# Moving the one-hot products of a head pair to its last double step, with three PSUM banks in turn until the weight decode ends

## The chip, the core and the metric

The kernel runs on one core of one Trainium2 chip. The metric is the device time of one execution in microseconds; lower is better. Three runs of the kernel before gave 1151.7, 1154.13 and 1152.92 us, so the median is 1152.92 us.

## What is computed

The reference is a routed attention followed by a feed-forward block. Every query and key is assigned to the nearest of 16 centroids of its head, and attention is limited to pairs of the same cluster:

```python
q_assign = np.argmax(np.einsum('bhsd,hcd->bhsc', q_n, c_n), axis=-1)
k_assign = np.argmax(np.einsum('bhsd,hcd->bhsc', k_n, c_n), axis=-1)
mask = q_assign[:, :, :, None] == k_assign[:, :, None, :]
scores = np.where(mask, scale * np.matmul(q, k.transpose(0, 1, 3, 2)), -1000000000.0)
# softmax over the last axis, times v; heads side by side give x of 3072 x 512
h = x @ w_in
g = h * np.clip(h + 3.0, 0.0, 6.0) / 6.0
return (g @ w_out).astype(np.float32)
```

There are 4 batches, 8 heads, 768 positions of 64 elements; w_in is 512 x 2048 and w_out 2048 x 512. Both weights arrive in 8-byte floating point, and the kernel turns them into 4-byte numbers on the chip (the "decode").

## The kernel before

**Pairs and double steps.** Two heads are worked on together. There are 16 such pairs. One pair has 12 score steps: two halves of the queries (`hf`) times six chunks of 128 keys (`j`). The main loop goes through them two at a time: a *double step* is n = 0, 2, 4, ... up to 190, and r = n mod 12 is its place in its pair. In a double step TensorE makes the scores of steps n and n+1 into the PSUM tile `ps` (L354: first `ps<-xf`, the q-k product in 4-byte numbers, then `ps<-xm`, the mask product in bf16), ScalarE takes the exponential (`ex`, L366), POOL adds the exponentials into `acc` (L370, L373), and TensorE multiplies those of the double step before by v (`pv`, L383).

**Division.** At r=2 and r=8 the function `divide` sums `acc` over the keys on TensorE (`pd`, L404), and VectorE takes the reciprocal (`rcp`, L408) and multiplies (`xT`, L409). One double step later ScalarE makes two range sums from rcp (`same` L417, `lack` L419).

**Preparing the next pair.** While pair g runs, pair g+1 is prepared: at r=0 and 2 q and k are transposed (`turn`: `pqk` L278, copied to `xf` L280), at r=4 come the cluster scores (`pcs` L291, copied to `cs`), at r=6 `route` transposes them (`pr` L302) and VectorE finds the winners and writes `one_hot` (L306 to L322). Then `route_turn(g, part)` turns the one-hot rows with an identity into `po` (L334, four products into one PSUM bank) and copies them to a third of `xm` (L338). Part 0 holds query chunks 0 to 3, part 1 query chunks 4 and 5 and key chunks 0 and 1, part 2 key chunks 2 to 5. Parts 0 and 1 are made at r=8, part 2 at r=10; `xm` is read by the mask products of the next pair from its r=0 on.

**PSUM.** `ps` has four banks, `pv` one. The tile pool `psum_t` has one bank and `psum_m` two. Short-lived tiles (pc, pqk, pcs, pr, po, pd) come from `scratch`: while `st["early"]` holds, they go to `psum_m` and `psum_t` in turn, after that to `psum_t` alone. `early` ends at n = READY = 52. From n=54 on `psum_m` also holds the feed-forward tiles `ph` and `py`.

**Feed-forward items.** From n=54 on the list `fill` gives TensorE items of the feed-forward block: `up` items (eight ph products, L434; then `t` on ScalarE, L441, and `gT` on VectorE, L443) and `down` items (eight py products, L456; after the fourth part the copy `y`, L462, on VectorE). How many are taken in a double step is fixed by `items_by`. Up to n = DECODED = 96 that is none or one; in the steps from 96 to 103 the rest of the first half; later two or three. Within a double step items and preparation alternate, an item first.

**Decode.** 32 chunks of the weights are decoded. Each takes two sums on ScalarE (`wsize`, L208, L211) and five operations on VectorE (`wtop`, `wunit`, and `w_in_sb` or `w_out_sb`, L217 to L231). Up to n=48 one chunk is decoded in every five steps, from there one in every double step, at its end. The last is done at n=94.

**Order.** The whole order is written out by hand (`tc.manual_schedule()`): each engine works through its list in the order in which the program issues it.

Of the kernel before, what the change touches and what calls it, by code (L numbers as in the profile page):

```python
# [116 lines left out]
def fast_path(ctx, tc, ok, q, k, v, centroids, moe_w_in, moe_w_out, out):  # L117


    nc = tc.nc  # L120
# [44 lines left out]
    def scratch(shape, name):  # L165

        st["scratch"] += 1
        if st["early"] and st["scratch"] % 3:
            return psum_m.tile(shape, F32, name=name, tag="m")
        return psum_t.tile(shape, F32, name=name, tag="t")  # L170
# [3 lines left out]
    def load(g, *names):  # L174
        if g >= NPAIR:
            return
        b, h = divmod(2 * g, H)
        for name in names:
            if name == "v":
                dst = st["v", g] = vp.tile([P, NCH, 2, D], F32, name="vt")  # L180
            elif name == "q":
                st["qk", g] = qkp.tile([P, 2, NCH, 2, D], F32, name="qk")
            if name != "v":
                dst = st["qk", g][:, "qk".index(name)]
            src = {"q": q, "k": k, "v": v}[name]
            for t in range(2):
                nc.sync.dma_start(dst[:, :, t], src[b, h + t].rearrange("(p j) d -> p j d", p=P))
# [9 lines left out]
    def load_weights(i):  # L197
        if i < len(chunks):
            st["raw", i] = rawp.tile([P, WC, 2], U32, name="raw")
            nc.sync.dma_start(st["raw", i], chunks[i][1])  # L200
# [37 lines left out]
    def constants():  # L238
        make_identity(nc, ident)
        nc.vector.tensor_copy(out=ident_q, in_=ident)  # L240
        nc.vector.tensor_scalar_mul(out=ident_k, in0=ident, scalar1=-FAR)
        for t in range(2):
            nc.vector.tensor_reduce(
                out=parity[:, t : t + 1],
                in_=ident.rearrange("p (h t c) -> p t h c", t=2, c=C)[:, t], axis=AX.XY, op=ALU.max,
            )
        for c in range(C):
            nc.gpsimd.memset(rank[:, c : c + 1], float(C - c))
        nc.gpsimd.memset(half_c, 0.5)
        nc.gpsimd.memset(low_c, 1.0 / BOUND)  # L250
        nc.gpsimd.memset(ones, 1.0)
        nc.gpsimd.memset(w_low, W_LOW)
        nc.gpsimd.memset(one_hot, 0.0)
# [17 lines left out]
    def turn(g, part):  # L271
        if part == 0:
            st["xf", g] = xp.tile([P, NC2, P], F32, name="xf")
        qk, xf = st["qk", g], st["xf", g]
        pt = scratch([P, NHC, P], "pqk")
        for i in range(NHC):
            j = part * NHC + i
            nc.tensor.transpose(out=pt[:, i], in_=qk[:, j // NCH, j % NCH], identity=ident)  # L278
        dst = xf[:, part * NHC : (part + 1) * NHC]
        nc.scalar.copy(out=dst, in_=pt)  # L280
        if part == 3:
            st.pop(("qk", g))
# [4 lines left out]
    def cluster_scores(g):  # L287
        c0, xf = (2 * g) % H * C, st["xf", g]
        ps = scratch([P, 512], "pcs")[:, 0 : NC2 // 4 * P]
        for a in range(4):  # L290
            nc.tensor.matmul(  # L291
                ps[a * 2 * C : (a + 1) * 2 * C], lhsT=cnT[:, c0 : c0 + 2 * C], rhs=xf[:, a::4],
                start=True, stop=True,
            )
        cs = st["cs", g] = rtp.tile([P, NC2 // 4, P], F32, name="cs")
        nc.scalar.copy(out=cs, in_=ps)

    def route(g):
        cs = st.pop(("cs", g))
        pr = scratch([P, NC2, 2, C], "pr")  # L300
        for i in range(NC2 // 4):
            nc.tensor.transpose(out=pr[:, 4 * i : 4 * i + 4], in_=cs[:, i], identity=ident)  # L302
        shape = [P, 2 * NC2, C]
        pr = pr.rearrange("p j t c -> p (j t) c")
        mx = rtp.tile([P, 2 * NC2], F32, name="mx")
        nc.vector.reduce_max(out=mx, in_=pr, axis=AX.X)  # L306
        tie = rtp.tile(shape, F32, name="tie")
        nc.vector.tensor_tensor(
            out=tie, in0=pr, in1=mx.unsqueeze(2).to_broadcast(shape), op=ALU.is_ge
        )  # L310

        nc.vector.tensor_tensor(  # L312
            out=tie, in0=tie, in1=rank.unsqueeze(1).to_broadcast(shape), op=ALU.mult
        )
        first = rtp.tile([P, 2 * NC2], F32, name="first")
        nc.vector.reduce_max(out=first, in_=tie, axis=AX.X)
        oh = one_hot.rearrange("p j (t c) -> p j t c", t=2)
        tie = tie.rearrange("p (j t) c -> p j t c", t=2)
        first = first.rearrange("p (j t) -> p j t", t=2)
        for a, op in ((0, ALU.is_equal), (1, ALU.not_equal)):  # L320
            sl = slice(a * NCH, (a + 1) * NCH)
            nc.vector.tensor_tensor(  # L322
                out=oh[:, sl, :, 0:C], in0=tie[:, sl],
                in1=first[:, sl].unsqueeze(3).to_broadcast([P, NCH, 2, C]), op=op,
            )

    def route_turn(g, part):
        if part == 0:
            st["xm", g] = xp.tile([P, NC2, P], BF16, name="xm")
        xm = st["xm", g]  # L330
        po = scratch([P, 4, P], "po")
        for i in range(4):
            j = part * 4 + i
            nc.tensor.matmul(  # L334
                po[:, i], lhsT=one_hot[:, j], rhs=(ident_q if j < NCH else ident_k),
                start=True, stop=True,
            )
        nc.scalar.copy(out=xm[:, part * 4 : part * 4 + 4], in_=po)  # L338


    def where(n):
# [3 lines left out]
    def scores_qk(n):  # L345
        g, hf, j = where(n)
        st["ps", n] = psum_s.tile([P, 2, 512], F32, name="ps")
        scores_part(n, st["xf", g], True)
# [129 lines left out]
    def prep_items(g, r):  # L478

        if g >= NPAIR:  # L480
            return []
        if r in (0, 2):
            return [lambda: turn(g, r), lambda: turn(g, r + 1)]
        return {
            4: [lambda: cluster_scores(g)],
            6: [lambda: route(g)],
            8: [lambda: route_turn(g, 0), lambda: route_turn(g, 1)],
            10: [lambda: route_turn(g, 2)],
        }.get(r, [])

    per_pair = 2 * NCH
# [8 lines left out]
    READY = per_batch + lag_d  # L500
    DECODED = per_batch + 2 * (NW - per_batch // 5) + 2
# [19 lines left out]
    with tc.manual_schedule():  # L521
        nc.scalar.dma_start(cen, centroids.rearrange("h c d -> (h c) d"))
        load(0, "q", "k")
        constants()
        load(0, "v")
        load_weights(0)
        centroid_norm()
        for part in range(4):
            turn(0, part)
        load(1, "q", "k")  # L530
        scores_qk(0)
        scores_qk(1)
        cluster_scores(0)
        route(0)
        for part in range(3):
            route_turn(0, part)

        for n in range(0, total + lag_d + 2, 2):
            g, r = divmod(n, per_pair)
            for i in (n, n + 1):  # L540
                if i < total:
                    scores(i)
            for i in (n - lag_v, n - lag_v + 1):
                if 0 <= i < total:
                    attn_v(i)
            for check in later:
                check()
            later = []
            m = n - lag_d + 1
            if m >= 0 and m % NCH == NCH - 1:  # L550
                later.append(divide(m))
            prep = prep_items(g + 1, r)
            if r == 4 and prep:
                prep.pop()()
            if n == READY:
                st["early"] = False
            if m >= 0 and m % per_batch == per_batch - 1:
                fill += ffn_items(m // per_batch)
            if r == 6:
                load(g + 2, "q", "k")  # L560
                load(g + 1, "v")
            want = items_by(n + 2) - done if n < total else len(fill)
            want = min(want, len(fill))
            done += want
            for i in range(max(len(prep), want)):
                if i < want:
                    fill.pop(0)()
                if i < len(prep):
                    prep[i]()
            for i in range(chunks_by(n), chunks_by(n + 2)):  # L570
                load_weights(i + 1)
                decode_weights(i)
            if n >= total:
                for check in later:
                    check()
                later = []
# [5 lines left out]
    for got, sums, high in ((good, totals, BOUND), (fit, w_totals, W_HIGH)):  # L582
        for a, bound in enumerate((high, 0.0)):
            nc.vector.tensor_scalar(
                out=got[:, a], in0=sums[:, a], scalar1=bound, scalar2=None, op0=ALU.is_le
# [372 lines left out]
```

## Time and profile before

| | |
|---|---|
| median of three runs | 1152.92 us |
| the profiled execution | 1153.49 us |
| its span in the profile | 1151.4 us |
| mean granted TensorE clock | 0.976 |
| TensorE busy | 1084.7 us (94%) |
| VectorE busy | 390.3 us (34%) |
| ScalarE busy | 381.6 us (33%) |
| POOL busy | 300.5 us (26%) |
| HBM traffic over the span | 36 GB/s |

PE is TensorE's matmuls, PEld its weight loads, DVE is VectorE, ACT is ScalarE, POOL is GpSimd. In the page's second part the span is cut into 40 equal slices of 28.8 us, and a digit is the busy share of a slice in tenths; PEclk is the TensorE clock that was granted, in tenths of full speed. A row of waits names who waited on which line, for whom, then total us, times, and the longest. A row of a timeline has the start in us, the duration in us, the engine, the line, the operation, and in brackets the idle time before it with what ended it. A row of windows has the stretch, its length, then each engine's busy time.

### The profile page before, as it was taken

How to read it: one execution, taken by the hardware profiler on the slowest of the kernel's cores; microseconds unless marked ns; L12 is line 12 of the kernel's file. 1: busy time of each engine (PE TensorE's matmuls, PEld its weight loads, DVE VectorE, ACT ScalarE, POOL GpSimd, SP SyncE). 2: the span in 40 equal slices, each digit the busy share in tenths (PEclk: the TensorE clock that was granted, in tenths of full speed). 3: DMA queues.
4: the chain of work that ended last, by engine and by line, in shares of the span. 5: the costliest groups of instructions: out<-in, count | busy, mean ns of one | idle time of the engine just before them, and what ended most of it. 6: DMA issues, size and time to landing. Idle time of an engine off the chain costs nothing.

```text
span 1151.4 us, 11063 instructions
## 1 busy us (share of the span) xinstructions
PE 1084.7 (94%) x4402; PEld 520.9 (45%) x4402; DVE 390.3 (34%) x499; ACT 381.6 (33%) x740; POOL 300.5 (26%) x187
## 2 busy tenths in 40 slices
PE   6999969778799999999999999999999999999996
PEld 3444424333344554554445544454445544544542
DVE  3699995655901111222122211223112210210210
ACT  4667656444520310333214322243123320210210
POOL 2677734343311100332223223233113320000000
PEclk8999989898999999999999999999999999999999
DMA  4333244132300100020020202010000000000000
GB/s 113 84 96 93 71 115 115 56 96 73 78 10 19 41 1 19 10 42 1 10 59 1 42 10 51 10 42 1 10 24 9 1 1 27 1 9 19 1 9 22
DMA packets 83532, 42.77 MB, mean 37 GB/s; under 512 B 76304, under 2 KB 76304, under 8 KB 83472
## 3 DMA queue, kind: packets, MB, share of 16 engines
q1 hardware_dynamic: 83328, 41.95, 14.1%
q8 instruction: 36, 0.59, 0.2%
q14 instruction: 24, 0.20, 0.1%
q10 hardware_dynamic: 144, 0.03, 0.0%
HBM read 35.68 MB, written 6.29 MB: 36 GB/s over the span
## 4 chain that ended last, share of the span: by engine, by line
PE 86%; DVE 12%; ACT 1%; issue 0%; POOL 0%; DVEq 0%; POOLq 0%
PE py L456 29%; PE ph L434 29%; PE ps L354 13%; PE pv L383 10%; DVE rcp L408 2%; PE pqk L278 2%; DVE one_hot L322 2%; PE pd L404 1%; PE po L334 1%; DVE w_in_sb L231 1%; DVE wunit L228 1%; DVE wunit L224 1%; DVE wtop L221 1%; PE pcs L291 1%; DVE tie L312 1%; DVE wtop L217 1%
## 5 line engine op out<-in xcount | busy, mean ns | idle before, releaser
L373 POOL TENSOR_TENSOR acc<-acc,ex 128x768 f32<-128x768 f32 x128 | 237.5, 1856 | 452.8 <-ACT ex L366 447.7
L434 PE MATMUL ph<-xT,w_in_sb 128*128 128x384 f32 x1024 | 347.3, 491 | 0.7 <-DVE rcp L408 0.7
L456 PE MATMUL py<-w_out_sb,gT 128*128 128x512 f32 x768 | 338.7, 595 | 0.0
L434 PEld LDWEIGHTS ph<-xT,w_in_sb 128*128 128x128 f32 x1024 | 188.9, 190 | 146.0 <-issue 27.1
L456 PEld LDWEIGHTS py<-w_out_sb,gT 128*128 128x128 f32 x768 | 142.8, 190 | 176.4 <-issue 175.4
L366 ACT ACTIVATE ex<-ps 128x768 f32<-128x768 f32 x192 | 150.9, 806 | 180.3 <-PE ps L354 179.9
L441 ACT ACTIVATE t<-ph,half_c 128x384 f32<-128x384 f32 x128 | 74.4, 581 | 368.2 <-PE ph L434 368.2
L443 DVE SCALAR_TENSOR_TENSOR gT<-t,ph 128x384 f32<-128x384 f32 x128 | 70.9, 554 | 312.1 <-ACT t L441 312.1
L354 PE MATMUL ps<-xf 64*128 64x384 f32 x768 | 175.8, 537 | 0.6 <-ACT ex L366 0.6
L383 PE MATMUL pv<-ex,vt 128*64 128x384 f32 x768 | 147.9, 507 | 0.0
L462 DVE COPY y<-py 128x512 f32<-128x512 f32 x24 | 16.6, 691 | 289.6 <-PE py L456 289.6
L370 POOL TENSOR_TENSOR acc<-ex 128x768 f32<-128x768 f32 x32 | 60.3, 1884 | 182.0 <-ACT ex L366 182.0
L408 DVE RECIPROCAL rcp<-pd 128x384 f32<-128x384 f32 x32 | 81.7, 2555 | 75.4 <-PE pd L404 75.3
L354 PEld LDWEIGHTS ps<-xf 64*128 64x128 f32 x768 | 67.0, 196 | 59.0 <-issue 42.3
L383 PEld LDWEIGHTS pv<-ex,vt 128*64 128x64 f32 x768 | 47.5, 139 | 85.2 <-issue 82.8
L354 PE MATMUL ps<-xm 64*128 64x384 bf16 x384 | 66.0, 338 | 0.7 <-ACT xm L338 0.7
L280 ACT COPY xf<-pqk 128x384 f32<-128x384 f32 x64 | 29.6, 479 | 77.1 <-PE pqk L278 77.1
L338 ACT CAST xm<-po 128x512 bf16<-128x512 f32 x48 | 27.4, 582 | 59.0 <-PE po L334 59.0
L334 PE MATMUL po<-ident_q,one_hot 128*128 128x128 bf16 x96 | 11.3, 244 | 37.6 <-DVE rcp L408 24.3
L334 PEld LDWEIGHTS <-one_hot 128*128 128x128 bf16 x192 | 14.6, 105 | 57.5 <-issue 37.4
L278 PE MATMUL pqk<-ident,qk 128*128 128x128 f32 x192 | 32.5, 293 | 6.6 <-ACT xf L280 3.9
L278 PEld LDWEIGHTS pqk<-ident,qk 128*128 128x128 f32 x192 | 24.1, 149 | 29.4 <-issue 14.2
(70 smaller groups left out, 460.2 us busy)
## 6 DMA issues: line engine op xcount, KB each, us to landing
raw<-in_moe_w_in_dram SPq DMA_DIRECT2D x16, 512.0 KB, 3.7
raw<-in_moe_w_out_dram SPq DMA_DIRECT2D x16, 512.0 KB, 3.5
qk<-in_q_dram SPq DMA_DIRECT2D x32, 192.0 KB, 3.4
qk<-in_k_dram SPq DMA_DIRECT2D x32, 192.0 KB, 4.1
vt<-in_v_dram SPq DMA_DIRECT2D x32, 192.0 KB, 4.1
out_dram<-y SPq DMA_DIRECT2D x24, 256.0 KB, 2.0
cen<-in_centroids_dram ACTq DMA_DIRECT2D x1, 32.0 KB, 1.8
```

Of the source, the lines that this page charges most:

```text
L278: nc.tensor.transpose(out=pt[:, i], in_=qk[:, j // NCH, j % NCH], identity=ident)
L334: nc.tensor.matmul(po[:, i], lhsT=one_hot[:, j], rhs=(ident_q if j < NCH else ident_k), start=True, stop=True,)
L354: nc.tensor.matmul(st["ps", n][:, t, 0:HALF], lhsT=x[r, NCH + j], rhs=x[r, hf * NHC : (hf + 1) * NHC], start=first, stop=not first,)
L366: nc.scalar.activation(out=ex, in_=sc, func=ACT.Exp, scale=SM_SCALE)
L370: nc.gpsimd.tensor_tensor(out=acc, in0=st["ex", n - 1], in1=ex, op=ALU.add)
L373: nc.gpsimd.tensor_tensor(out=acc, in0=acc, in1=ex, op=ALU.add)
L383: nc.tensor.matmul(pv[t * D : (t + 1) * D], lhsT=vt[:, j, t], rhs=ex[:, t], start=(j == 0), stop=(j == NCH - 1),)
L408: nc.vector.reciprocal(out=rcp, in_=pd)
L434: nc.tensor.matmul(hh, lhsT=w_in_sb[:, kt, f * P : (f + 1) * P], rhs=xT[:, kt, hf * HALF : (hf + 1) * HALF], start=(kt == 0), stop=(kt == ...
L441: nc.scalar.activation(out=t, in_=hh, func=ACT.Relu, bias=half_c, scale=1.0 / 6.0)
L443: nc.vector.scalar_tensor_tensor(out=gT, in0=t, scalar=1.0, in1=hh, op0=ALU.min, op1=ALU.mult)
L456: nc.tensor.matmul(py, lhsT=st["g", f][:, i * P : (i + 1) * P], rhs=w_out_sb[:, f], start=(f == 0), stop=(f == NFT - 1),)
```

## The change

Three things are edited. `route_turn` is called for all three parts at r=10, and for none at r=8. The copy of part 1 goes to VectorE; those of parts 0 and 2 stay on ScalarE. And `early` ends at n = DECODED (96) instead of READY (52), so that scratch tiles go round three banks for that much longer, in which the feed-forward tiles use two of them too. The call of all three parts for the first pair, ahead of the loop, gets VectorE's copy as well.

```diff
                 po[:, i], lhsT=one_hot[:, j], rhs=(ident_q if j < NCH else ident_k),
                 start=True, stop=True,
             )
-        nc.scalar.copy(out=xm[:, part * 4 : part * 4 + 4], in_=po)
+        dst = xm[:, part * 4 : part * 4 + 4]
+        if part == 1:
+            nc.vector.tensor_copy(out=dst, in_=po)
+        else:
+            nc.scalar.copy(out=dst, in_=po)
...
             6: [lambda: route(g)],
-            8: [lambda: route_turn(g, 0), lambda: route_turn(g, 1)],
-            10: [lambda: route_turn(g, 2)],
+            10: [lambda: route_turn(g, 0), lambda: route_turn(g, 1), lambda: route_turn(g, 2)],
         }.get(r, [])
...
-            if n == READY:
+            if n == DECODED:
                 st["early"] = False
```

## The prediction

> **What bounds the kernel now.** I read the busy table and the 40 slices first, then TensorE's waits, then the windows by stage, then the timeline at the pair boundaries, where the change acts.
>
> ```profile
> PE 1084.7 (94%) x4402; PEld 520.9 (45%) x4402; DVE 390.3 (34%) x499; ACT 381.6 (33%) x740; POOL 300.5 (26%) x187
> PE   6999969778799999999999999999999999999996
> DVE  3699995655901111222122211223112210210210
> PEclk8999989898999999999999999999999999999999
> ```
> TensorE is full from slice 11 on. Before that it has holes, VectorE is the busy neighbour, and the granted clock dips after each hole.
>
> ```profile
> PE po L334 <- DVE rcp L408: 24.3, 4, 8.1
> PE po L334 <- DVE one_hot L322: 12.0, 6, 3.0
> PE pqk L278 <- ACT xf L280: 3.9, 6, 0.7
> PE po L334 <- ACT xm L338: 2.7, 4, 0.7
> PE pqk L278 <- DVE rcp L408: 2.7, 1, 2.7
> ```
> All waits of size concern the scratch tiles. These windows put them in stages (span, PE busy, DVE busy, ACT, POOL, PEclk):
>
> ```profile
> 36.00:129.30 93.30, 84.26 (x539) 37.65 (x539) 85.68 (x74) 63.35 (x131) 63.49 (x33) 0.96 0.31 78
> 172.90:322.70 149.80, 122.46 (x605) 57.79 (x602) 97.35 (x134) 80.30 (x176) 55.74 (x31) 0.91 0.30 80
> 322.70:1140.00 817.30, 817.30 (x2938) 396.74 (x2935) 151.34 (x216) 195.01 (x350) 144.99 (x80) 1.00 0.07 17
> ```
> So before 323 us a removed hole is time won. After 323 us TensorE has no hole at all, and any new one is time lost.
>
> I name double steps by n (0, 2, ...); counting the ps groups puts n=12 at 45.7 us, 24 at 74.5, 36 at 101.6, 48 at 128.6, 60 at 172.1, 72 at 220.1, 84 at 273.5, 96 at 321.9. A boundary is the scores of n=12, 24, ...: their xm product needs parts 0 and 1, while part 2 is wanted one step later. So today part 2 alone is made in the last step, and nothing waits for it.
>
> **The change, stage by stage.** It adds no arithmetic: 16 of 48 copies go from ScalarE (582 ns) to VectorE. The nearest row is `y<-py`, a VectorE copy of 128x512 out of PSUM, 691 ns. I take 0.69 us (0.58 would change the sum by 1 us). No DMA is moved, and SP and POOL get the same lists. Behind the moved copy VectorE has that step's decode and the next rcp, behind ScalarE's copies come the decode's sums and the next exp; where part 1's products are late, these wait too, which no row shows: 0 while TensorE is the late one anyway, at most one copy (0.7 us) at a boundary.
>
> *Boundaries 108 to 180, after the decode (7 pairs).* One bank is left for scratch tiles here, and each of these last steps has two FFN items. Built, the order is item, part 0, item, part 1, part 2: nothing stands between part 1's copy and part 2's products in the same bank. Scores and the rest of TensorE's list queue behind that wait.
>
> ```profile
> 478.26 0.39 PE L334 MATMUL po<-ident_k,one_hot 128*128 128x128 bf16 x4
> 478.46 0.58 ACT L441 ACTIVATE t<-ph,half_c 128x384 f32<-128x384 f32 x1 [2.25 <-PE ph L434]
> 479.07 0.55 DVE L443 SCALAR_TENSOR_TENSOR gT<-t,ph 128x384 f32<-128x384 f32 x1 [5.70 <-ACT t L441]
> ```
> In 4 of the 7 pairs the second item is an `up`. VectorE takes its gT first: products start at 0, gT ends at 1.36, the copy ends at 2.08, TensorE resumes at 2.14 instead of 0.32: 1.8 us. In 3 pairs it is a `down` part without a copy: 0.39 + 0.03 + 0.69 + 0.05 - 0.32 = 0.85. Sum 4 x 1.8 + 3 x 0.85 = 9.8 us, all on the path; at r=8 nothing was lost before, so nothing comes back.
>
> The clock adds to it. These two slices say where it drops:
>
> ```profile
> 38.00:41.40 3.40, 1.78 (x18) 1.06 (x18) 3.40 (x3) 1.44 (x3) 1.88 (x2) 1.00 0.00 0
> 41.40:44.80 3.40, 3.40 (x14) 1.20 (x12) 3.26 (x4) 3.37 (x9) 1.33 (x1) 0.50 0.00 0
> ```
> A 3.4 us slice in which TensorE was busy 1.78 us is followed by one at half clock; the slice 96.0 to 99.4, busy 1.96, is not. An `up` wait of 1.75 us idle, if it falls nearly whole into one such slice (about 57 in 100), leaves 1.66 busy, and the next slice costs half of 3.4 us: 4 x 0.57 x 1.7 = 3.9 us (0 to 6.8). Stage sum +13.7.
>
> The Trainium skill, "TensorE: Matmul & The Clock Gate", section "Why this matters for your kernels", says otherwise: only idle gaps above about 3 us should cost the clock. By it this term is 0 and the whole sum 3.9 us lower. The slice above had 1.62 us of idle, split in two, so I follow the row.
>
> *Boundaries 12, 24, 36 (before the FFN).* The one_hot waits at r=8 (12.0 less 3.0 at the start) vanish: po comes a step later. But xm now waits for the last step's copies, and both engines reach them late. ScalarE has same and lack (L417, L419) ahead, which need rcp: part 0 is copied 1.8 us after rcp ends (74.50 to 76.22 in the trace). VectorE has rcp, xT and, at 12, one decode ahead.
>
> ```profile
> 40.09 2.54 DVE L408 RECIPROCAL rcp<-pd 128x384 f32<-128x384 f32 x1
> 43.67 2.19 DVE L221 SCALAR_TENSOR_TENSOR wtop<-raw,wtop 128x512 uint32<-128x512 uint32 x1
> 45.89 1.91 DVE L224 TENSOR_SCALAR wunit<-wtop 128x512 uint32<-128x512 uint32 x1
> ```
> The two decode ops above stretch from 0.69 and 0.43 because POOL's additions run beside them (43.47 to 47.52). A decode takes 2.9 us alone, and about 1.5 more for each op so blocked.
> - 12: rcp ends 42.63, xT waits for POOL until 44.4, decode to 47.3, copy to 48.05, against 46.42 today: +1.6 (0.6 with no block). The idle brings one half-clock slice: +1.5.
> - 24: the decode before rcp ran unblocked (68.98 to 72.03) because the one_hot wait had starved POOL. Without that wait the additions fall on it: rcp ends 74.5 to 77.5, xm follows 1.8 later, 76.3 to 79.3 against 75.26: +1.0 to +4.1. I take 3.0, nearer the blocked rows as POOL will be running, and 1.4 for the clock.
> - 36: rcp ends 100.12, xm 101.9 to 102.25, against 102.33: 0.
> Sum +7.5 (1.6 to 8.6). The start wins 0.2: two copies run side by side.
>
> *Boundaries 48 and 60.* At 48 rcp ends 127.1; xT, a decode and the copy put xm at 131.5 to 132.2, against 129.32. At 60 VectorE is one unbroken chain. Today xm follows the end of rcp by 8.5 us; then by xT 0.56 + gT 0.55 + decode 2.9 + copy 0.7 + gaps = 4.85, so -3.65 if rcp stays. It does not: TensorE comes 5 us late out of 48 (wait and half clock), and POOL blocks decodes that now run beside it, about +4.7. I take +1 (-3.6 to +4).
>
> *Boundaries 72, 84, 96: the gain.* The po <- rcp waits vanish at r=8.
>
> ```profile
> 204.98 0.41 DVE L217 TENSOR_SCALAR wtop<-raw 128x512 uint32<-128x512 uint32 x1
> 207.96 2.55 DVE L408 RECIPROCAL rcp<-pd 128x384 f32<-128x384 f32 x1
> 210.56 0.58 PE L334 MATMUL po<-ident_q,one_hot 128*128 128x128 bf16 x4 [5.24 <-DVE rcp L408]
> 220.86 0.33 PE L354 MATMUL ps<-xm 64*128 64x384 bf16 x2
> ```
> From the end of rcp to xm today: 10.35, 11.4, 10.8 us. After: xT, gT, decode, gT, copy = 5.4, 4.85, 5.4. That is -17.0 if rcp stays. But exp and POOL's additions now run while VectorE decodes ahead of rcp; by the blocked rows this moves rcp by 1.8, 3.2, 1.7: +6.7. New idle before each boundary (on gT or rcp, whose bank a scratch tile or an `up` now shares) brings half clock again: 0.5 + 2.0 + 1.8 = +4.3. The three banks also free the turns: pqk waits of 0.7, 0.6, 3.3 and 1.2 go, with one half-clock slice (1.2): -7.0. Sum -13.0 (-24 with no block, -8 with three more blocked ops).
>
> **Sum.** 13.7 + 7.5 - 0.2 + 1.0 - 13.0 = +9.0 us. The profiled execution took 1153.49 us, of which the span is 1151.4; the shown median is 1152.92, so I predict 1162 us. Ends: 9.8 + 1.6 - 0.2 - 3.6 - 24 = -16.4, and 16.6 + 8.6 - 0.2 + 4 - 8 = +21.
>
> **Rivals.**
> - *VectorE keeps up (faster).* One mechanism: whether POOL's additions block the decode ops at 48 to 96. If they don't, the gain is 24 + 3.6 and 24 costs only 1.0: -24 - 3.6 + 13.7 + 1.6 + 2.9 - 0.2 = -9.6, 1143 us. I count ten such blocks (1 at 12, 2 at 24, 3 at 60, 1, 2 and 1 later); between 9.0 and -9.6 the sign turns where about half of them stay away. For it: VectorE is idle 35% of 172.9 to 322.7. Against: the stretched rows recur wherever POOL is busy. Chance 0.18.
> - *Wash.* Stage gain 22 against the same losses: within 0.2%, 2.3 us, which is about what a measurement of this kernel can tell from no change. Chance 0.08.
> - *Heavier.* `up` tiles share two banks with scratch tiles, so ph waits for a gT that sits behind a decode; each of five boundaries loses another 2 to 3 us with its clock slice: +20, 1173 us. For it: the built order puts three ph in a row into one bank at n=60 to 64. Against: gT there had idle time before it (5 to 7 us). Chance 0.19.
> - *The change doesn't do what it says*: excluded by the built order; the tiles stand in three banks up to n=94, and part 1's copy stands on VectorE 16 times.
> My forecast (1153 to 1168): 0.55. The range for 8 in 10 reaches from 1146, which leaves out most of the first rival's own spread, to 1174. Faster by over 0.2%: 0.17; within: 0.09; slower: 0.74.
>
> **What would show it.** In the waits, po <- rcp falls from 24.3 to under 8 us, po <- one_hot to about 3 (the start), and new rows stand: ps or po <- VectorE's xm copy, near 10 us after 323 us (po, 7 times, four near 1.8) and more before. The span from the scores of n=60 to those of 96 shrinks from 150 to about 137 us, that from 12 to 48 grows by about 5. PEclk shows single dips after slice 11. I am wrong if the late po waits are near 0.2 us, if the clock doesn't dip beside them, or if decode ops keep their 0.4 and 0.7 us while POOL is busy.

## The result and the profile after

The changed kernel takes 1160.92 us (median of 4 runs, 1159.53 to 1162.33) against 1152.31 us for the kernel before beside it (4 runs, 1150.65 to 1154.13): 1.0074 times as long, 95% interval 1.0054 to 1.0095. Its profiled execution took 1162.33 us, with a span of 1160.4 us and a mean granted clock of 0.971.

First the busy table and the 40 slices of the page after; a slice is 29.0 us here.

```profile
PE 1088.9 (94%) x4402; PEld 522.7 (45%) x4402; DVE 398.4 (34%) x515; ACT 375.0 (32%) x724; POOL 300.7 (26%) x187
PE   6879897997999999999999999999999999999996
DVE  4497777877901120222122301323112210210210
PEclk9889998998999999999999999999999999999999
```

VectorE has 16 instructions more, ScalarE 16 fewer: the moved copies. The holes of TensorE are still in the first eleven slices. After them the granted clock is full until the last 6 us, though the waits below say that new holes stand there. Those of TensorE's waits that concern the moved products (who waited on which line, for whom, total us, times, longest):

```profile
PE po L334 <- DVE rcp L412: 21.2, 6, 6.8
PE ps L358 <- DVE xm L340: 10.5, 5, 4.0
PE po L334 <- DVE xm L340: 8.9, 7, 1.6
PE po L334 <- DVE gT L447: 5.0, 2, 3.5
PE po L334 <- DVE one_hot L322: 4.4, 3, 3.0
```

The one_hot row shrank to little more than the start (from 12.0). The rcp row hardly did (from 24.3). Two rows on VectorE's copy of `xm` are new: one for the scores (ps), with 3.99 us at 12, 3.86 at 48 and three short ones, and one for part 2's products (po) after 323 us, seven times.

How much each boundary moved is read from the first exp of double step n in both timelines (us, after minus before):

| n | 12 | 24 | 36 | 48 | 60 | 72 | 84 | 96 | 108 | 132 | 156 | 180 |
|---|---|---|---|---|---|---|---|---|---|---|---|---|
| difference | +0.6 | +7.3 | +11.0 | +15.4 | +11.3 | +7.3 | +1.8 | -1.0 | +0.7 | +3.2 | +5.8 | +8.3 |

So the change loses 15.4 us up to the scores of n=48, wins 16.4 from there to 96, and loses 9.3 again from 96 to 180. The last 0.7 us of the 9.0 by which the span grew come after the last exp. Single boundaries are known less well than to the tenth: e1 below runs the program of before up to n=52 and is 2.2 us earlier at 48, and e3 below runs that of after up to 96 and is 3.8 us earlier there. Differences of that size are not the edit's.

The timeline at one of the four late boundaries with an `up` item:

```profile
479.77 0.58 ACT L445 ACTIVATE t<-ph,half_c 128x384 f32<-128x384 f32 x1 [1.80 <-PE ph L438]
480.38 0.56 DVE L447 SCALAR_TENSOR_TENSOR gT<-t,ph 128x384 f32<-128x384 f32 x1 [2.30 <-ACT t L445]
480.85 0.68 DVE L340 CAST xm<-po 128x512 bf16<-128x512 f32 x1
481.59 0.38 PE L334 MATMUL po<-ident_k,one_hot 128*128 128x128 bf16 x4 [1.64 <-DVE xm L340]
```

VectorE's list has gT ahead of the copy, gT waits for ScalarE's `t`, and part 2's products wait 1.64 us for the one bank. And two early boundaries, 24 (above the dots) and 12 (below):

```profile
78.27 2.55 DVE L412 RECIPROCAL rcp<-pd 128x384 f32<-128x384 f32 x1
80.85 0.52 ACT L421 ACTIVATE same<-rcp 128x384 bf16<-128x384 f32 x1 [8.93 <-DVE rcp L412]
80.87 0.59 PE L334 MATMUL po<-ident_k,one_hot 128*128 128x128 bf16 x4 [6.76 <-DVE rcp L412]
81.97 1.05 ACT L342 CAST xm<-po 128x512 bf16<-128x512 f32 x2
...
46.09 0.68 DVE L340 CAST xm<-po 128x512 bf16<-128x512 f32 x1
46.83 0.50 PE L358 MATMUL ps<-xm 64*128 64x384 bf16 x2 [3.99 <-DVE xm L340]
```

At 24 two things stand behind the same rcp at once: TensorE's products of part 2, whose bank the denominators `pd` hold until rcp has read it, and ScalarE's `same` and `lack`, with the copies of parts 0 and 2 in line after them. At 12 the scores wait 3.99 us for the VectorE copy, which stands behind a whole decode.

### The profile page after: what moved, and what is told of

It reads as the page before. It is cut to its first block, busy times and chain, and to the rows that moved or that the text cites. A ratio compares the mean times of both kernels' runs of the same rounds, so it can differ in the third digit from the quotient of the medians.

```text
span 1160.4 us, 11063 instructions
## 1 busy us (share of the span) xinstructions
PE 1088.9 (94%) x4402; PEld 522.7 (45%) x4402; DVE 398.4 (34%) x515; ACT 375.0 (32%) x724; POOL 300.7 (26%) x187
## 3 DMA queue, kind: packets, MB, share of 16 engines
q1 hardware_dynamic: 83328, 41.95, 14.1%
## 4 chain that ended last, share of the span: by engine, by line
PE 82%; DVE 16%; ACT 1%; issue 0%; POOL 0%; DVEq 0%; POOLq 0%
PE py L460 29%; PE ph L438 28%; PE ps L358 11%; PE pv L387 9%; DVE rcp L412 3%; DVE one_hot L322 2%; PE pqk L278 2%; DVE wunit L228 2%; PE pd L408 1%; DVE wtop L221 1%; DVE wunit L224 1%; DVE w_in_sb L231 1%; DVE wtop L217 1%; DVE xT L413 1%; DVE tie L312 1%; PE pcs L291 1%
## 5 line engine op out<-in xcount | busy, mean ns | idle before, releaser
L387 PE MATMUL pv<-ex,vt 128*64 128x384 f32 x768 | 151.7, 518 | 0.0
L358 PEld LDWEIGHTS <-xm 64*128 64x128 bf16 x384 | 20.0, 97 | 40.6 <-DVE xm L340 14.8
L334 PE MATMUL po<-ident_k,one_hot 128*128 128x128 bf16 x96 | 11.5, 238 | 25.6 <-DVE rcp L412 11.0
```

Of the source, the lines that this page charges most:

```text
L358: nc.tensor.matmul(st["ps", n][:, t, 0:HALF], lhsT=x[r, NCH + j], rhs=x[r, hf * NHC : (hf + 1) * NHC], start=first, stop=not first,)
L387: nc.tensor.matmul(pv[t * D : (t + 1) * D], lhsT=vt[:, j, t], rhs=ex[:, t], start=(j == 0), stop=(j == NCH - 1),)
```

## The experiments

**Which part of the change does what (e1, e2).** The three edits come apart: three banks without the move and the VectorE copy, and the other way round.

```diff
e1, from the kernel before:
-            if n == READY:
+            if n == DECODED:
e2, from the kernel after:
-            if n == DECODED:
+            if n == READY:
```

> The kernel before with one edit alone: scratch tiles go round three banks until n=96; the one-hot products stay at r=8, 8 and 10, and all copies on ScalarE. As built, part 0 has another bank than pd at n=68 and 80 and the same one at n=56 and 92. Theory (the po waits on rcp before 323 us are a matter of the bank that pd holds): two of the four waits (5.2 and 8.1 us at 68 and 80) shrink to a wait on one_hot of 0 to 2.6 us, the other two stay, the pqk waits shrink: about 1142 us (1135 to 1147). Rival (VectorE's chain sets the pace whatever the banks are, and the wait comes back on ps, ph or xm): within 4 us of 1152. After 323 us no new wait in either.

> The changed kernel without the banks: all three parts at r=10 and part 1's copy on VectorE, but scratch tiles have one bank from n=52 on. Theory: the losses at boundaries 12 to 36 (11.0 us in the changed kernel) and after 323 us (9.3 us) stay as they are; from 48 to 96 the three parts go through one bank one after the other, part 2 behind a VectorE copy that stands behind a decode, so the gain of 12.3 us shrinks to 3 to 9: about 1166 us (1160 to 1171). Rival (the gain comes from the move to r=10 and not from the banks): the gain stays, 1158 to 1162 us.

Measured: e1 1131.35 us, 0.982 times the kernel before (0.9804 to 0.9836); e2 1175.12 us, 1.0199 times (1.0184 to 1.0215). Before is 1152.77 in this group. The signs were right and both sizes far too small: the banks alone win 21 us where 11 were expected, the move with its copy loses 22 where 13 were. The banks carry nearly all of the gain, and the move takes it back: with the banks given, it costs 1160.92 - 1131.35 = 29.6 us. Between 60 and 96, where the move was to pay, e2 wins 0.9 us. In e1's waits:

```profile
PE po L334 <- DVE one_hot L322: 14.2, 8, 3.0
PE po L334 <- DVE rcp L408: 12.9, 2, 7.6
PE pqk L278 <- DVE rcp L408: 0.9, 1, 0.9
PE pqk L278 <- ACT xf L280: 0.7, 1, 0.7
```

Two of the four rcp waits are gone without any move, since the other turns of the three banks do not meet `pd`.

**Where by stage (e3, e4).** The change stands only for the pairs for which COND holds; all others have the old order of the products and ScalarE's copies. g is the pair prepared, and the code is shortened.

```diff
+            8: [] if COND else [part 0, part 1],
+            10: [all three parts] if COND else [part 2],
...
+        if part == 1 and COND:
             nc.vector.tensor_copy(out=dst, in_=po)
e3: COND is g < 9       e4: COND is 5 <= g < 9
```

> The changed kernel, with the schedule of before (parts 0 and 1 at r=8, part 2 at r=10, ScalarE's copies) for the seven pairs prepared after n=96. Theory: the 9.3 us that the changed kernel loses from step 96 to step 180 are the seven waits of part 2's products on part 1's VectorE copy and nothing else; they go: 1151.6 us (1150 to 1153), and from the scores of step 96 to those of step 180 it takes what before took, 558.6 us. Rival (part of the loss is a later state of the pipeline, carried in from the first stages): 1153 to 1157 us.

> The new schedule and VectorE's copy only for the four pairs prepared from n=48 to 94 (boundaries 60, 72, 84, 96), the schedule of before for all others, three banks until n=96. Theory (stages add up): the 11.0 us at 12 to 36 and the 4.4 us at 48 are not lost, the 9.3 us after 323 us are not lost, and the gain of 12.3 us at 72 to 96 stays; boundary 60, which won 4.1 us after a late 48, gives 0 to 4: about 1138 us (1135 to 1143). Rival (the gain at 72 to 96 is in part the early losses given back, since VectorE had drained its decodes by then): 1144 to 1152 us.

Measured: e3 1151.01 us (0.9984, 0.9972 to 0.9996), e4 1137.69 us (0.9876, 0.9858 to 0.9894). The median falls by 9.9 us, where 9.3 were told, and e3's timeline shows nothing lost from 96 to 180 (-4.77 against before at both), so the late boundaries cost what the timeline said, 9.3. e4 is a hit too, but e1 without any move is 6.3 us faster still: where the move was thought to pay, the banks were paying.

**What in the move costs (e5, e6, e7).** Three steps, each on top of the one before: part 1's copy back on ScalarE; part 2 kept out of pd's bank at the boundaries 12 to 48 (`own` names the pool); `same` and `lack` issued after the products and copies.

```diff
e5:
-        if part == 1:
-            nc.vector.tensor_copy(out=dst, in_=po)
-        else:
-            nc.scalar.copy(out=dst, in_=po)
+        nc.scalar.copy(out=dst, in_=po)
e6, too:
+        own = {1: "t", 2: "t", 3: "m", 4: "t"}.get(g) if part == 2 else None
+        po = scratch([P, 4, P], "po", own)
e7, too:
-            for check in later:
-                check()
-            later = []
+            due, later = later, []
...
             for i in range(max(len(prep), want)):
...
+            for check in due:
+                check()
```

> The change with part 1's copy put back on ScalarE; banks and the move to r=10 stay. Theory VectorE-copy: the copy stands behind the rows that VectorE has queued (decode at boundaries 12 and 48, gT at the late up boundaries), so the scores' wait of 3.99 us at 12 falls to about 1.4 and the one of 3.86 us at 48 likewise (some 2.6 us each and up to 1.4 of half clock each), late up waits fall from 1.7 to about 1.15 and down waits from 0.85 to 0.75 (4 x 0.55 + 3 x 0.1 = 2.5 us): 1160.9 - 8.5 = 1152.5 (1150 to 1156). Rival, the move alone: all three parts stand after rcp and behind ScalarE's same and lack, whatever engine copies part 1: 1159.5 to 1161.5. Both expect boundary 24 to keep its 6.8 us wait.

> As e5, and part 2's products of pairs 12 to 48 are kept out of the bank that the denominators pd use. Theory bank: what holds boundaries 24 and 36 is that bank (waits for rcp of 6.76 and 2.18 us), so they lose 8 to 9 us less than with e5: 1144 (1142 to 1147). Rival, ScalarE's queue: the copies stand behind same and lack, which wait for the same rcp, so the wait only turns from po to ps (ps for xm): within 1.5 us of e5, 1151 to 1154. I lean to the rival: in the trace of the change the xm copies at boundary 24 come at 81.97, behind same at 80.85 and lack at 81.37.

> As e6, and same and lack are issued after the step's products and copies, so nothing between the products and the scores waits for rcp at the early boundaries. Both theories of e6 are cured: boundaries 12 to 48 go at least as early as in the kernel before (differences of 0 to -2 us), 1160.9 - 8.5 (e5) - 9 = about 1141 (1137 to 1145), with the late boundaries still +6.9 us over before. If the move itself costs by something else (one_hot blocked by POOL, VectorE being late), it stays above 1148.

Measured, with before at 1152.5: e5 1144.85 us (0.9941, 0.9926 to 0.9956); e6 1150.1 (0.9987, 0.9977 to 0.9996); e7 1133.82 (0.9835, 0.9815 to 0.9856; its five runs lie from 1130.78 to 1137.38). By boundary, against before (the profiled executions):

| n | 12 | 24 | 36 | 48 | 60 | 72 | 84 | 96 | 180 |
|---|---|---|---|---|---|---|---|---|---|
| after | +0.6 | +7.3 | +11.0 | +15.4 | +11.3 | +7.3 | +1.8 | -1.0 | +8.3 |
| e5 | -2.3 | +2.2 | +5.6 | +8.1 | +2.9 | -2.5 | -9.7 | -15.1 | -9.0 |
| e6 | -3.2 | +3.3 | +7.0 | +11.3 | +4.3 | -0.9 | -8.2 | -13.6 | -7.5 |
| e7 | -2.8 | -0.5 | -0.1 | -1.5 | -6.0 | -11.6 | -18.5 | -22.0 | -15.9 |
| e1 | -2.0 | -2.3 | -2.2 | -2.2 | -4.1 | -8.8 | -21.9 | -23.0 | -23.0 |

e5: the VectorE copy costs 16.1 us in all, twice what was expected, and the move with ScalarE's copies the other 13.5 (1144.85 - 1131.35). In the profiled runs e5 is 14.1 us ahead of the change by n=96, most boundaries adding 1 to 3 us, and gains 3.2 more late. At a late `up` boundary ScalarE's copy has only `t` ahead of it, and the wait is 0.92 instead of 1.64 us:

```profile
465.65 0.58 ACT L442 ACTIVATE t<-ph,half_c 128x384 f32<-128x384 f32 x1 [1.80 <-PE ph L435]
466.13 0.58 ACT L339 CAST xm<-po 128x512 bf16<-128x512 f32 x1
466.76 0.38 PE L334 MATMUL po<-ident_k,one_hot 128*128 128x128 bf16 x4 [0.92 <-ACT xm L339]
```

e6 settles between the two causes at 24 and 36. The bank theory (1144) falls: out of pd's bank the wait stays and changes its name, as the copies themselves stand behind `same` and `lack`. The same two waits in e5 (the first two rows) and in e6 (the last two); the 9.0 us are those at 24:

```profile
PE po L334 <- DVE rcp L409: 21.9, 6, 6.8
PE po L334 <- ACT xm L339: 7.1, 9, 0.9
PE po L335 <- ACT xm L340: 26.3, 13, 9.0
PE po L335 <- DVE rcp L410: 8.4, 2, 4.9
```

Its median is 5.2 us above e5's, more than the 1.5 allowed, while its profiled execution (1146.42 us) is only 1.5 above; that difference is left open. e7 then takes the sums out of the way, and the loss of +7.0 at 36 goes to -0.1. It came out 7 us better than expected; e5, on which the sum was built, had already come out 8 us better. Of the 12.8 us by which e7 is ahead of e6 at 48, 8.4 are left at 96. So at the early boundaries ScalarE's list, with the sums ahead of the copies, is enough by itself to hold the loss; whether pd's bank alone would hold it too was not tried. e7's late boundaries still lose 6.1 us, which is what sets it behind e1 in the table.

**Whether e1's two remaining rcp waits can go (e8, e12).** e8 keeps the products of the pairs at 60 and 96 in the bank that pd doesn't use; e12 holds the decode issued at r=6 back until after the denominators of r=8.

```diff
e8, from e1:
+        po = scratch([P, 4, P], "po", g in (5, 8))    # True: psum_t
e12, from e1:
+            if held and r != 6:
+                decode_weights(held.pop())
             for i in range(chunks_by(n), chunks_by(n + 2)):
                 load_weights(i + 1)
-                decode_weights(i)
+                if r == 6:
+                    held.append(i)
+                else:
+                    decode_weights(i)
```

> e1 (the kernel before with three banks until DECODED, no move, no VectorE copy) with the products of pairs 60 and 96 kept in the bank that pd does not use: there e1 still waits for rcp 7.58 and 5.36 us. Theory bank: both waits go, and only the copy between parts of one bank (0.7 us each) stays: 1131.3 less 6 to 11 us = 1123 (1120 to 1126). Rival, VectorE is what is late in that stage: the wait comes back at the next gT, pqk or pd, 1129 to 1132.

> e1 with the decode that is issued at r = 6, between one_hot and rcp on VectorE, held back until after the denominators of r = 8. Theory rcp behind the decode: the two waits po for rcp of e1 (7.6 and 5.3 us) shrink by the 2.9 us of a decode each, and the half-clock slices behind them by some: 1131.4 - 5.8 - 0 to 3 = 1124 (1121 to 1127). Rival, VectorE is full there whatever the order: the wait comes back at gT, pd or pqk, 1129 to 1133.

Measured: e8 1131.63 us (0.9822, 0.9805 to 0.9838), no different from e1. The two waits of po for rcp are gone, and this stands in their place:

```profile
PE pqk L278 <- DVE rcp L408: 8.6, 2, 4.6
```

The rival fits: the wait for VectorE comes back under another name, and nothing is won. e12 took 1139.07 us (0.9887, 0.9872 to 0.9902), worse than e1 and outside of both expectations. Its po for rcp did fall, from 12.9 to 3.0 us, but its decode became slower: the five operations of a chunk sum to 5.10 us in the mean between 36 and 322 us, against 4.58 in e1. Of the 155 decode operations there 45 take 1.5 us or more, against 34 in e1. That two chunks in a row now run beside POOL's additions, and that this costs the 8 us, was argued, not tried.

**Whether POOL's additions stretch the decode (e10, e11).** The kernels before and after without the additions for j over 1, so that the softmax denominators lack four of the six key chunks; only their times count here.

```diff
-        elif j > 1:
-            acc = st["acc", g, hf]
-            nc.gpsimd.tensor_tensor(out=acc, in0=acc, in1=ex, op=ALU.add)
```

> The kernel before without GpSimd's additions of the exponentials for j over 1 (the softmax denominator is then the sum of the first two key tiles only), to be held against e11. Theory POOL blocks the decode: no decode operation is stretched to 1.9 to 2.2 us any more, and the boundaries up to 96 come earlier by some of it: 1140 (1130 to 1148). Rival, POOL is beside the point: 1150 to 1153.

> The change without GpSimd's additions for j over 1, as in e10. Theory POOL blocks the decode: the loss at boundary 24 falls from 6.75 us to 1 to 2, the gain between 72 and 96 grows from 12.3 to 17 or more, the late stage stays at +9.3; e11 less e10 is -3 us (-10 to +1). Rival, POOL is beside the point: e11 less e10 is +6 to +10 as with the additions.

Measured: e10 1120.67 us (0.9728, 0.9713 to 0.9743), e11 1113.91 us (0.9671, 0.9655 to 0.9686). Without the additions the change wins 6.8 us; with them it loses 8.6. The groups of VectorE's third decode operation between 36 and 322 us (busy, then mean ns of one, then idle), in before and in e10:

```profile
L224 DVE TENSOR_SCALAR wunit<-wtop 128x512 uint32<-128x512 uint32 x31 | 26.7, 862 | 1.1
L224 DVE TENSOR_SCALAR wunit<-wtop 128x512 uint32<-128x512 uint32 x31 | 13.2, 427 | 1.1
```

The mean halves, and all five operations of a chunk go from 4.30 to 2.98 us. Of the 155 decode operations there, 28 take 1.9 us or more in before and 1 in e10. The loss from 12 to 24 is 6.75 us with the additions and 2.9 - 1.7 = 1.2 us as e11 less e10; from 60 to 96 the gain is 12.3 and 19.4 us; from 96 to 180 the loss is 9.3 in both. So the expectation for e11 holds in each part, while e10 itself won 31 us where 13 were told.

**Where the clock drops (e9).** Part 1's VectorE copy is made twice at the late boundaries.

```diff
-            nc.vector.tensor_copy(out=dst, in_=po)
+            for _ in range(2 if g >= 9 else 1):
+                nc.vector.tensor_copy(out=dst, in_=po)
```

> The change with part 1's VectorE copy made twice for the pairs from n = 108 on, so each late wait grows by one copy (0.7 us): up waits 1.75 to 2.45, down waits 0.85 to 1.55. Theory waits only: +7 x 0.7 = 4.9 us, 1165.8 (1165 to 1167). Theory clock by slice (a slice in which TensorE is busy about half or less is followed by one at half clock): at 2.45 us of idle the four up slices, 0.52 busy now, fall to about 0.3 to 0.4, and each costs 1.7 us more: +4.9 + 6.8 = 1172.6, or 1169 if two of four slices are split. In the Trainium skill, TensorE: Matmul & The Clock Gate, section Why this matters for your kernels, gaps under about 3 us cost no clock, which is the first number.

Measured: 1169.73 us (1.0138, 1.0116 to 1.0159), 8.8 above the change. From 96 to 180 it loses 17.8 us, against 9.3: 8.5 more, of which the seven longer waits are 5.1 (the row in after, then in e9):

```profile
PE po L334 <- DVE xm L340: 8.9, 7, 1.6
PE po L334 <- DVE xm L341: 14.0, 7, 2.4
```

The other 3.4 are two slices at half clock; one follows the wait at 480, the other that at 620. Windows of 3.4 us (length, PE busy, PEld, DVE, ACT, POOL, granted clock, DMA share, GB/s), after ahead of e9:

```profile
479.10:482.50 3.40, 1.76 (x14) 0.99 (x15) 1.16 (x2) 1.07 (x2) 0.00 (x0) 1.00 0.00 0
482.50:485.90 3.40, 3.40 (x20) 1.43 (x17) 0.00 (x0) 2.20 (x4) 1.12 (x1) 1.00 0.02 5
```

```profile
478.30:481.70 3.40, 1.03 (x10) 0.51 (x9) 1.85 (x3) 0.58 (x1) 0.00 (x0) 1.00 0.00 0
481.70:485.10 3.40, 3.40 (x16) 1.49 (x13) 0.00 (x0) 1.40 (x2) 0.00 (x0) 0.51 0.02 5
```

With 1.76 us busy the next slice keeps its clock; with 1.03 it does not, after one wait of 2.37 us. The other two long waits of e9 fell into two slices each, and none of these cost the clock. Its five runs spread from 1164.75 to 1170.42 us, the two shortest at a mean clock of 0.973 and 0.974 against 0.967 and 0.968; only one of the longer ones was profiled, so how many slices a run loses is open.

## Why the prediction was right, and where it was not

Forecast 1162, measured 1160.92. The sum of +9.0 us is the growth of the span (1160.4 - 1151.4), but that it fits to the tenth is luck: two of its terms, the late clock (3.9 us too much) and boundary 36 (3.6 too little), were wrong and cancelled.

- *Late waits, 9.8 us:* right. The seven steps of the timeline are four of 1.70 and three of 0.85 us, 9.3 in all, and e3 without them loses nothing from 96 to 180.
- *Late clock, 3.9 us:* wrong, it is 0. The step that failed took one row (1.78 us busy, next slice at half clock) as the rule for an `up` slice. Three of the four `up` waits fell whole into one slice, which was about as busy (1.76 us in the row above), and not one cost the clock. Slices about half busy went either way (see the last section), so one such row could not give the sign. The Trainium skill, "TensorE: Matmul & The Clock Gate", section "Why this matters for your kernels", with its gaps of about 3 us, would have given this term rightly; e9 shows that the rule is not the measure either, as a wait of 2.37 us did halve the clock.
- *Boundaries 12, 24, 36, +7.5 (with the start +7.3):* up to 24 the sum is right, +7.3, and its split is not. At 12 only 0.6 us stand, as the decode there ran unblocked (0.41 to 0.69 us each), which the prediction priced at 0.6 beside its 1.6; from there to 24 it is 6.75, where 1.5 + 3.0 + 1.4 = 5.9 were told. The step that failed is 36, priced at 0 because rcp was taken to end where it ended before. It ended 3.7 us later, counted from the exp of 24. Part of it (1.6 us) is the prediction's own mechanism of boundary 24, which it had not applied here: without the one_hot wait POOL's additions run unbroken, and one_hot takes 3.16 us instead of 1.52. Before, then after:

```profile
96.13 1.52 DVE L322 TENSOR_TENSOR one_hot<-tie,first 128x192 bf16<-128x192 f32 x2
100.12 3.91 POOL L373 TENSOR_TENSOR acc<-acc,ex 128x768 f32<-128x768 f32 x2 [2.95 <-ACT ex L366]
105.51 3.16 DVE L322 TENSOR_TENSOR one_hot<-tie,first 128x192 bf16<-128x192 f32 x2
102.56 7.77 POOL L377 TENSOR_TENSOR acc<-acc,ex 128x768 f32<-128x768 f32 x4 [0.33 <-ACT ex L370]
```

- *Boundaries 48 and 60, +1.0:* +0.3 as a sum, out of +4.4 and -4.1.
- *Boundaries 72 to 96, -13.0:* -12.3 by the timeline. But the reason given, products that no longer wait for rcp because they come a step later, isn't it. At r=10 they still wait for rcp, 5.39 us at 60 and 4.87 at 84; e2, which moves them without the banks, wins 0.9 us between 60 and 96, and e1, which keeps them at r=8, wins 18.9, where 7.0 were put down to the banks. Its banks alone take 11.4 us off po for rcp (24.3 to 12.9) and 5.0 off pqk (6.6 to 1.6), and the move on top gave 18.9 - 12.3 = 6.6 back. The size was right by luck, the edit that it was put down to was not.
- *The first rival, VectorE keeps up:* its deciding point was the right one. Take the additions away and the change wins 6.8 us (e10, e11), where the rival said 9.6. The condition wasn't met: of the 155 decode operations between 36 and 322 us 22 take 1.9 to 2.3 us in the kernel after, each beside an addition, as this one does ahead of boundary 84 (0.69 us unblocked). 11 others ran for more than half of their time beside an addition and kept their length.

```profile
265.61 2.18 DVE L228 SCALAR_TENSOR_TENSOR wunit<-raw,wunit 128x512 f32<-128x512 uint32 x1
```

- *Heavier:* a wait of that kind exists, but it is po and not ph that waits for gT (5.0 us), at two places (72 and 84) instead of five.
- *What would show it:* po for rcp was to fall under 8 and is 21.2, the wrong item: early, at 60 and at 84 part 2 or part 0 stand in pd's bank. The late row (8.9 us, 7 times), 60 to 96 (136.6 us, 137 told) and the stretched decodes came as told. 12 to 48 grew by 14.8 and not by 5: 6.8, 3.6 and 4.4 us up to 24, 36 and 48. The clock did not dip after slice 11, which was named as a way of being wrong.

## What to carry to other kernels

Take a change of several edits apart before pricing it as one: here one line (the banks until the decode ends) is worth 21 us, and the move beside it cost 30. When work moves to a later step, read every engine's list at the new place, the copies' too: what stood behind nothing may now stand behind an unrelated wait (`same` and `lack` behind rcp, a copy behind gT), and changing the bank then only renames the wait. Of all that ran, the kernel before with three banks until DECODED (e1, 1131.35 us) is the fastest of those that leave nothing out, with e8 beside it and e7 close behind.

## What the runs showed of the hardware

Cut every profile into slices of 3.41 us at the phase in which the granted clock changes, and take the slices from 20 us to 1100 us that ran at full clock. TensorE busy for under 0.42 of the slice: 72 of 72 were followed by a slice at half clock. From 0.54 to 0.75: none of 80. Between 0.42 and 0.54: 13 of 38, so there the busy share alone does not tell. (Counted in one way; a slightly different phase of the slices moves a few of those near the bounds.) Idle time in one gap can be followed by half clock (e9 at 478.3, 2.37 us), and so can idle time in two (before, 38.0 to 41.4, 1.62 us in all).

POOL's additions cost VectorE more than expected. They stretch a decode chunk from 2.98 to 4.30 us in the kernel before, and leaving most of them out makes that kernel 31 us faster (1152.01 to 1120.67), though its additions also stand ahead of `pd` and so of rcp; how the 31 us divide between the two was not tried. The Trainium skill, "SBUF — State Buffer", section "SBUF: two separate sides", tells of a port pair that VectorE and GpSimd lock by turns; the rows of 0.43 and 0.69 us that become 1.9 to 2.3 us beside additions of 1.9 us agree with that.
